# Nine buffers of arriving expert weights, taken from a free queue, in place of a ring of four

## The chip, the cores and the metric

The kernel runs on one core of one Trainium2 chip. The metric is the device time of one execution, in microseconds (us), lower is better. Before the change the median of three runs is 621.47 us (620.87 to 623.8). An execution with the hardware profiler gave the trace that is read here.

## The reference

Three parts follow one another. First an attention over 768 positions (2 batches, 8 heads of width 64) with 4 sink columns and a window of 128. Its output, 1536 tokens of 512 numbers, goes through an MLP with 2048 hidden units. The tokens then go to one of 8 experts each:

```
logits = x @ w_gate; e = argmax(logits); gate = softmax(logits)[e]
position of the token in its expert's queue (at most capacity = 384 = 1536/8*2)
h = relu(disp @ w1[e])          # 512 -> 1024
y = h @ w2[e]                   # 1024 -> 512
out[token] = gate * y           # zero for tokens beyond the capacity
```

All matrices of the experts are float32. Each expert has 2 MB in w1 and 2 MB in w2.

## The kernel before, in words

Attention, MLP and experts run one after the other; the order of the instructions of every engine is written out by hand (the scheduler is in manual mode for all five engines), and each engine runs its list in order. The change lies in the expert stage and in the loading of its weights.

**Weights.** The weights of an expert come in eight pieces of 128 x 1024 float32 (512 KB each): four of w1 ("up"), four of w2 ("down"); 64 pieces in all, in the order of `raw_src` (line 1126). A piece arrives in one of the four quarters of `raw_all` by a DMA on SP's queue (`raw_loads`, line 1160). `expert_split` (line 1141) then makes two tiles of it: ACT copies it to a rounded high part (line 1145), and VectorE (DVE) subtracts that from the piece for the low part (line 1147); for the last piece of an expert, GpSimd (POOL) subtracts in DVE's place. The two tiles lie in slots that were used by the earlier stages (32 slots, so the split weights of two experts fit). A quarter of `raw_all` is free again when its subtraction is done, so a load can be at most four pieces ahead of the splits. SP's queue holds nothing but these loads in this stage, and SP takes no part in the conditional blocks.

**Chunks.** An expert's tokens are worked on in chunks of 128: chunk 0 without a condition, chunks 1 and 2 in nested conditional blocks (`guard`, line 1196; `further_chunks`, line 1259), which PE, ACT, DVE and POOL run or skip by the counted tokens. A chunk is: fetch of the rows from the table `xs` in DRAM by POOL's queue (`fetch`, line 403); `turn_in` (line 411): four transposes on TensorE (PE), a copy on ACT, a subtraction on DVE; `expert_up` (line 1203): 24 matmuls and two ReLUs on ACT into `hh`; `turn_hidden` (line 1219): eight transposes, two copies on ACT into `hth` and two subtractions on DVE into `htl`; `expert_down` (line 1236): 24 matmuls, a scaling on DVE, and a scatter to the output by POOL. Three products (high-high, low-high, high-low) make each matrix product.

**Order in one expert e** (the loop at line 1285), as each engine sees its share of it:

```
splits_to((e + 1) * PER)              # four splits, down weights of e
expert_up(e, 0)
turn_in(e + 1, 0); turn_in(e, 1)
fetch(e + 2, 0); fetch(e + 1, 1)
splits_to((e + 1) * PER + PW1)        # four splits, up weights of e + 1
expert_down(e - 1, 0)
turn_hidden(e, 0)
further_chunks(e, 1)                  # conditional: chunks 1 and 2
fetch(e + 1, 2)
```

`raw_loads` is called after each group of splits. For expert 1 the groups are shifted by one piece, and for the last expert `turn_hidden(7, 0)` comes before `expert_down(6, 0)`. With the inputs measured, the conditional chunks that run are 1 and 2 of expert 0, 1 of expert 1, 1 of expert 3, and 1 and 2 of expert 6; experts 2, 4, 5 and 7 skip theirs. Chunk 0 of expert 0 is worked off among the last steps of the MLP.

**Room.** The pool `ep` (line 1182) opens when the MLP's pools are closed, in their memory. It has two buffers a tile unless a tile says otherwise: `hh` 2, `xha`/`xla` (chunk 0) and `xhb`/`xlb` (chunks 1, 2) 2 each, `hth` and `htl` 3 each.

Of the kernel before, what the change touches and what calls it, by code (L numbers as in the profile page):

```python
# [9 lines left out]
F32 = mybir.dt.float32  # L10
F32R = mybir.dt.float32r
# [24 lines left out]
def attention_mlp_moe_kernel(  # L36
# [17 lines left out]
    nc = tc.nc  # L54
    P = 128
    B, _, _, S = q.shape
    _, NG, _, GH, NQ, D1 = v.shape
    D = D1 - 1
    H = NG * GH
    NT, DM = out.shape  # L60
    DFF = w_in.shape[1]
    E = w_gate.shape[2]
    F = w1.shape[2]
# [7 lines left out]
    if n_sink == 0 and window == 0:  # L71
# [20 lines left out]
        out=lt, in_=lt, pattern=[[1, P]], compare_op=ALU.is_gt, fill=0.0,  # L92
# [22 lines left out]
    SW = 1024  # L115
# [69 lines left out]
    raw_all = rawpool.tile([P, 4 * SW], I32, name="raw_all")  # L185
# [215 lines left out]
    rows, tx, ep = {}, {}, []  # L401
# [9 lines left out]
    def turn_in(e, c, pt=None, th=None, tl=None):  # L411
        r = rows.pop((e, c))
        if pt is None:
            tag = "a" if c == 0 else "b"
            pt = next_bank("t")
            th = ep[0].tile([P, DM], F32R, tag=f"xh{tag}", name=f"xh{e}_{c}")
            tl = ep[0].tile([P, DM], F32R, tag=f"xl{tag}", name=f"xl{e}_{c}")
        for kk in range(KD):
            nc.tensor.transpose(pt[:, kk * P:(kk + 1) * P], r[:, kk * P:(kk + 1) * P], ident)
        nc.scalar.copy(th, pt)  # L420
        nc.vector.tensor_sub(tl, pt, th.bitcast(F32))
        tx[e, c] = (th, tl)

    def turn_in_slot(e, c, tag, pt):
        x = slot(tag)
        turn_in(e, c, pt, x[:, :DM], x[:, DM:])

    def first_chunk():
# [30 lines left out]
        for o in range(0, F, 512):  # L459
# [8 lines left out]
            yield  # L468
        splits_to(PER + PW1)
        raw_loads()  # L470
        got.extend((r, who, ht, downs))

# [17 lines left out]
    def mlp_steps():  # L490
# [30 lines left out]
        for bl in range(NBLK):  # L521
            last = bl == NBLK - 1
            if last:
                raw_loads()
                splits_to(1)
            for f in range(KF):
                n = bl * len(worder) + f
                conv = convert_at(n)
                next(conv, None)
                for ph in mlp_up(bl, f, wts[bl, "wi", f // FG]):  # L530
                    yield
                if last and f == KF - 1:
                    down_to(0)
                elif len(pending) == LAG:
                    routing = lower() or routing
                pending.append((bl, f, mlp_act(bl, f, ph, split_at(n), conv)))
                if f % 2 and bl == 1:
                    next(n_fill, None)
                if routing is not None and f >= 2:
                    next(routing, None)  # L540
                if last and f >= 2 and f % 2 and f < KF - 1:
                    splits_to(min(split_n[0] + 1, PER))
                    raw_loads()
                if last and f in (KF - 5, KF - 2):
                    next(first)
# [62 lines left out]
    with ExitStack() as actx:  # L608
# [19 lines left out]
        for i in range(NQ):  # L628
# [5 lines left out]
            m = ap_c.tile([P, w], F32, name=f"mask{len(masks)}")  # L634
# [3 lines left out]
            for (d, sink), o in zip(row, offs):  # L638
# [3 lines left out]
                if d * P - (P - 1) < 0:  # L642
                    nc.gpsimd.affine_select(
                        out=mb, in_=mb, pattern=[[-1, P]], compare_op=ALU.is_ge,
                        fill=NEG, base=d * P, channel_multiplier=1,
                    )
                if d * P + (P - 1) > window - 1:
                    nc.gpsimd.affine_select(
                        out=mb, in_=mb, pattern=[[1, P]], compare_op=ALU.is_ge,
# [264 lines left out]
        for n in range(nu + 11):  # L914
# [35 lines left out]
            if n == nu - EARLY:  # L950
                nc.vector.tensor_scalar(
                    out=nalpha, in0=alpha_sb, scalar1=-1.0, scalar2=None, op0=ALU.mult
# [23 lines left out]
    def moe_slot():  # L976
        moe_pos[0] += 1
        return slot(moe_tags[(moe_pos[0] - 1) % len(moe_tags)])
# [144 lines left out]
    w2_v = w2.rearrange("e (j p) d -> e p j d", p=P)  # L1123
    experts = {}

    raw_src = []

    def raw_of(m):
        return raw_all.bitcast(F32)[:, m % 4 * SW:(m % 4 + 1) * SW]

    for e in range(E):
        experts[e] = ([], [])
# [7 lines left out]

    def expert_split(m):
        _, dst, cut = raw_src[m]
        raw = raw_of(m)
        hi, lo = moe_slot(), moe_slot()
        nc.scalar.copy(hi, raw)  # L1145
        eng = nc.gpsimd if m % PER == PER - 1 and m > 2 * PER else nc.vector
        eng.tensor_sub(lo, raw, hi.bitcast(F32))  # L1147
        for o in range(0, SW, cut):
            dst.append([t[:, o:o + cut] for t in (hi, lo)])

    split_n, raw_n = [0], [0]

    def splits_to(n):
        while split_n[0] < min(n, len(raw_src)):
            if split_n[0] == raw_n[0]:
                raw_loads()
            expert_split(split_n[0])
            split_n[0] += 1

    def raw_loads():  # L1160
        while raw_n[0] < min(split_n[0] + 4, len(raw_src)):
            src = raw_src[raw_n[0]][0]
            nc.sync.dma_start(
                out=raw_of(raw_n[0]).rearrange("p (a b) -> p a b", a=src.shape[1]), in_=src
            )
            raw_n[0] += 1

    if not ahead:
# [18 lines left out]
    def next_bank(nm):  # L1187
        n = bank_n[nm] = bank_n.get(nm, -1) + 1
        return banks[nm][n % len(banks[nm])]

    counts, hid, hts = {}, {}, {}

    meta = ep[0].tile([P, E * NCH, 2], F32, name="meta", bufs=1)
# [9 lines left out]
    def expert_up(e, c):  # L1203
        ups = experts[e][0]
        x = tx.pop((e, c))
        h = ep[0].tile([P, F], F32, tag="hh", name=f"hh{e}_{c}")
        for o in range(0, F, 512):
            ph = next_bank("u")
            for kk in range(KD):
                for n, (xl, wl) in enumerate(((0, 0), (0, 1), (1, 0))):  # L1210
                    nc.tensor.matmul(  # L1211
                        ph, x[xl][:, kk * P:(kk + 1) * P],
                        ups[kk][wl][:, o:o + 512],
                        start=(kk == 0 and n == 0), stop=(kk == KD - 1 and n == 2),
                    )
            nc.scalar.activation(h[:, o:o + 512], ph, AF.Relu)  # L1216
        hid[e, c] = h

    def turn_hidden(e, c, between=None):
        h = hid.pop((e, c))  # L1220
        th = ep[0].tile([P, F], F32R, tag="hth", name=f"hth{e}_{c}", bufs=3)
        tl = ep[0].tile([P, F], F32R, tag="htl", name=f"htl{e}_{c}", bufs=3)
        hts[e, c] = (th, tl)
        for o in range(0, F, 512):
            w = slice(o, o + 512)
            pt = next_bank("t")
            for j in range(o // P, o // P + 4):
                nc.tensor.transpose(
                    pt[:, j * P - o:(j + 1) * P - o], h[:, j * P:(j + 1) * P], ident
                )  # L1230
            nc.scalar.copy(th[:, w], pt)
            nc.vector.tensor_sub(tl[:, w], pt, th.bitcast(F32)[:, w])
            if o == 0 and between:
                between()
# [24 lines left out]
    def further_chunks(e, c):  # L1259

        if c == NCH:
            return
        if NCH > 3:
            for c in range(1, NCH):
                with guard(e, c):
                    if c > 1:
                        fetch(e, c)
                        turn_in(e, c)
                    expert_up(e, c)
                    turn_hidden(e, c)  # L1270
                    expert_down(e, c)
            return
        with guard(e, c):  # L1273
            expert_up(e, c)
            turn_hidden(e, c, (lambda: turn_in(e, c + 1)) if c + 1 < NCH else None)
            expert_down(e, c)
            further_chunks(e, c + 1)

    nc.gpsimd.dma_start(
        out=meta, in_=xs.rearrange("(n p) d -> p n d", p=P)[:, :, DM:XW]  # L1280
# [4 lines left out]
    for e in range(E):  # L1285

        splits_to((e + 1) * PER - (e == 1))
        if e:
            expert_up(e, 0)
# [10 lines left out]
        if e == E - 1:  # L1300
            turn_hidden(e, 0)
# [84 lines left out]
```

## Time and profile before

| | |
|---|---|
| median of 3 runs | 621.47 us (620.87 to 623.8) |
| the profiled execution, its time | 619.51 us |
| its span, first to last instruction | 617.7 us |
| mean granted TensorE clock | 0.992 of full |
| attention, MLP and chunk 0 of expert 0 | 0 to 426 us |
| the rest of the expert stage | 427 to 612 us |
| PE busy over the span | 95% |
| weight loads of the experts | 64 of 512 KB, issued from 185.5 to 567.9 us |

How it is read: the profile gives, for each engine, what it ran and when, and for an instruction that began after an idle time, how long that was and what ended it. Times are us from the start of the span. A timeline row is start, duration, engine, line, operation, tile written <- tiles read, shape, count of instructions merged into the row, and in brackets the idle time before it and its releaser. "ACTq L1273" is ACT's instruction queue at the end of the loop body that holds the conditional blocks, not a computing instruction. The names `et`, `eo`, `es` are the PSUM banks of the expert stage, and `wi`, `wo`, `x`, `r` the slots of the split weights.

### The profile page before, as it was taken

The page shows a single profiled execution, that of the slowest core. Times are in us where ns is not written, and L with a number is a line of the kernel's source. Part 1 is how long each engine was busy: PE and PEld are TensorE (multiplying, and loading weights), DVE is VectorE, ACT ScalarE, POOL GpSimd, SP SyncE. Part 2 cuts the span into 40 slices and gives each one's busy share as a digit, 9 for nine tenths or more (in the row PEclk, how much of TensorE's full clock was granted, in tenths as well). Part 3 has the DMA queues.
Part 4 walks back from the last instruction along what each step waited for, and adds up shares of the span by engine and source line. Part 5 has one row for each costly group of instructions (what it writes and reads, how often), then busy time and mean ns, then how long its engine had stood idle before and what let it go on. Part 6 is the DMA issues. An engine that isn't in the chain of part 4 may idle for free. (4 is left out here: it accounts for less than half of the span.)

```text
span 617.7 us, 9115 instructions
## 1 busy us (share of the span) xinstructions
PE 589.9 (95%) x3230; PEld 493.4 (80%) x3230; DVE 400.6 (65%) x788; ACT 348.4 (56%) x642; POOL 98.3 (16%) x134
## 2 busy tenths in 40 slices
PE   7999999999999999999999999999999899889994
PEld 6999998888677888888899898876776687678783
DVE  6678788499998454444466787965146874766250
ACT  5668787475655544335465686835246564666330
POOL 5012333200000000002000110213120332222031
PEclk9999999999999999999999999999999999899999
DMA  7979731225568000001000012426345892999000
GB/s 221 303 238 298 206 122 69 69 84 190 162 195 324 1 1 0 2 17 52 0 2 1 36 49 69 154 73 216 99 129 179 289 329 90 315 319 314 24 21 34
DMA packets 32404, 81.76 MB, mean 132 GB/s; under 512 B 3574, under 2 KB 4134, under 8 KB 32352
## 3 DMA queue, kind: packets, MB, share of 16 engines
q1 hardware_dynamic: 28208, 69.54, 35.0%
q0 software_dynamic: 4144, 11.53, 5.4%
q8 instruction: 31, 0.51, 0.3%
q14 instruction: 21, 0.17, 0.1%
HBM read 66.65 MB, written 16.29 MB: 134 GB/s over the span
## 5 line engine op out<-in xcount | busy, mean ns | idle before, releaser
L350 PE MATMUL h<-x,r 128*128 128x512 f32 (+1 forms) x768 | 149.3, 341 | 3.2 <-DVE r L262 3.1
L350 PEld LDWEIGHTS h<-x,r 128*128 128x128 f32 x768 | 120.1, 189 | 22.3 <-DVE r L262 5.2
L381 PE MATMUL acc<-r,gh 128*128 128x512 f32 x384 | 120.6, 395 | 0.0
L381 PEld LDWEIGHTS acc<-r,gh 128*128 128x128 f32 x384 | 69.9, 188 | 14.4 <-ACT gh L370 0.3
L381 PE MATMUL acc<-r,gl 128*128 128x512 f32 x192 | 75.9, 395 | 0.0
L363 DVE SCALAR_TENSOR_TENSOR g<-gn,nalpha,g 128x512 f32<-128x512 f32 (+1 forms) x64 | 39.4, 616 | 47.5 <-ACT g L362 47.5
L722 PE MATMUL s<-ka,qa 128*128 128x260 f32 x192 | 59.8, 398 | 4.4 <-DMA qa<-in_q_dram 4.0
L361 ACT ACTIVATE gn<-h 128x512 f32<-128x512 f32 (+1 forms) x64 | 31.3, 490 | 53.5 <-PE h L350 53.2
L832 PEld LDWEIGHTS o<-vr,pT 128*128 128x128 f32 x352 | 55.6, 192 | 4.8
L1104 POOL DMA_INDIRECT xs<-x,slot_i x12 | 14.1, 1179 | 271.2 <-DVE run L1120 151.2
L262 DVE TENSOR_TENSOR r<-wo,r 128x1024 fp32r<-128x1024 f32 x31 | 38.0, 1224 | 27.6 <-ACT r L259 27.4
L832 PE MATMUL o<-vr,pT 128*128 128x65 f32 x352 | 53.6, 251 | 0.0
L1216 ACT ACTIVATE hh<-et 128x512 f32<-128x512 f32 x26 | 15.3, 596 | 59.5 <-PE et L1211 53.0
L741 ACT ACTIVATE p<-sx,mn 128x260 f32<-128x260 f32 (+1 forms) x96 | 42.9, 487 | 9.3 <-DVE mn L737 8.8
L259 ACT CAST r<-wo 128x1024 fp32r<-128x1024 f32 (+1 forms) x33 | 33.8, 1025 | 22.7 <-PE acc L381 21.7
L754 PE MATMUL pt<-ident,p 128*128 128x128 f32 x176 | 46.2, 278 | 0.0
L737 DVE CUSTOM_DVE_ANT_0 sx<-s,mask 128x260 f32<-128x260 f32 (+1 forms) x96 | 36.9, 401 | 13.7 <-PE s L722 8.5
L1147 DVE TENSOR_TENSOR wo<-raw_all,wi 128x1024 fp32r<-128x1024 f32 x29 | 39.5, 1392 | 9.2 <-ACT wi L1145 8.0
L370 ACT CAST gh<-g 128x512 fp32r<-128x512 f32 (+1 forms) x64 | 33.0, 515 | 21.3 <-DVE g L363 21.1
L381 PEld LDWEIGHTS acc<-r,gl 128*128 128x128 f32 x192 | 36.1, 188 | 8.6 <-DVE gl L373 0.2
L262 DVE TENSOR_TENSOR r<-wi,r 128x1024 fp32r<-128x1024 f32 x30 | 36.7, 1223 | 3.6 <-ACT r L259 3.4
L1145 ACT CAST wi<-raw_all 128x1024 fp32r<-128x1024 f32 x32 | 32.6, 1051 | 10.6 <-DMA raw_all<-in_w_dram 10.0
(192 smaller groups left out, 1106.9 us busy)
## 6 DMA issues: line engine op xcount, KB each, us to landing
raw_all<-in_w_dram SPq DMA_DIRECT2D x64, 512.0 KB, 5.2
raw_all<-in_w_in_dram SPq DMA_DIRECT2D x8, 1024.0 KB, 5.4
raw_all<-in_w_out_dram SPq DMA_DIRECT2D x8, 1024.0 KB, 5.0
xs<-r SPq DMA_DIRECT2D x8, 771.0 KB, 11.6
rows<-xs POOLq DMA_DIRECT2D x20, 256.0 KB, 4.7
vr<-in_v_dram SPq DMA_DIRECT2D x4, 780.0 KB, 4.9
out_dram<-fill SPq DMA_DIRECT2D x2, 1536.0 KB, 11.5
ka<-in_k_dram SPq DMA_DIRECT2D x7, 396.0 KB, 8.8
```

Source lines behind the costliest of these rows:

```text
L259: nc.scalar.copy(hi[:, x], w[:, x])
L262: eng.tensor_sub(lo[:, x], w[:, x], hi.bitcast(F32)[:, x])
L350: nc.tensor.matmul(ph[:, :TB], wi[wl][:, kk, f0:f0 + P], xT_at(kk, tok, TB, xl), start=(n == 0), stop=(n == 3 * KD - 1),)
L363: nc.vector.scalar_tensor_tensor(out=g, in0=gn, scalar=nalpha[:, f:f + 1], in1=g, op0=ALU.mult, op1=ALU.add)
L370: nc.scalar.copy(gh, g)
L381: nc.tensor.matmul(acc[t], g[a][:, t * P:(t + 1) * P], wo[w][:, f % FG, :], start=(f == 0 and x == 0), stop=(f == KF - 1 and x == 2),)
L722: nc.tensor.matmul(s[:, o:o + w], st.qa[:, h, toks], st.ka[:, c:c + w], start=True, stop=True, skip_group_check=True,)
L737: nc.vector.tensor_tensor_reduce(out=x[:, :w], in0=u.s[h][:, :w], in1=m[:, :w], scale=-scale, scalar=BIG, op0=ALU.add, op1=ALU.min, accum_ ...
L741: nc.scalar.activation(t.p[:, u.ii, h, :w], x[:, :w], AF.Exp, bias=t.mn[:, c:c + 1], scale=-1.0)
L754: nc.tensor.transpose(pt[:, c * P:(c + 1) * P], t.p[:, u.ii, h, u.offs[n]:u.offs[n] + P], ident,)
L832: nc.tensor.matmul(t.o[:, 2 * u.ii + h, :], u.pT[:, w], vr[:, hv * NQ + j, :], start=(not sg and n == 0), stop=(n == len(js) - 1), skip_gr ...
L1147: eng.tensor_sub(lo, raw, hi.bitcast(F32))
```

## The change

Five more buffers for arriving pieces (`more_raw`, 20 KB a partition) are allocated in `ep`, and the ring of four (piece m in quarter m mod 4) becomes a list of free buffers: a load takes the first free one, a split gives its buffer back to the end. Up to the opening of `ep` there are four buffers, as before; from there on nine. To make room, `hh`, `xha` and `xla` get one buffer instead of two, and `hth` and `htl` go from three buffers shared by all chunks to one for chunk 0 and one for chunks 1 and 2 (the other way round for the last expert): 16 KB a partition are given up.

```diff
-            th = ep[0].tile([P, DM], F32R, tag=f"xh{tag}", name=f"xh{e}_{c}")
-            tl = ep[0].tile([P, DM], F32R, tag=f"xl{tag}", name=f"xl{e}_{c}")
+            th = ep[0].tile([P, DM], F32R, tag=f"xh{tag}", name=f"xh{e}_{c}", bufs=1 + (c > 0))
+            tl = ep[0].tile([P, DM], F32R, tag=f"xl{tag}", name=f"xl{e}_{c}", bufs=1 + (c > 0))
...
+    MORE_RAW = 5
     raw_src = []
-    def raw_of(m):
-        return raw_all.bitcast(F32)[:, m % 4 * SW:(m % 4 + 1) * SW]
+    raw_free = [raw_all.bitcast(F32)[:, n * SW:(n + 1) * SW] for n in range(4)]
+    raw_at = {}
...
     def expert_split(m):
         _, dst, cut = raw_src[m]
-        raw = raw_of(m)
+        raw = raw_at.pop(m)
+        raw_free.append(raw)
...
     def raw_loads():
-        while raw_n[0] < min(split_n[0] + 4, len(raw_src)):
+        while raw_free and raw_n[0] < len(raw_src):
             src = raw_src[raw_n[0]][0]
-            nc.sync.dma_start(
-                out=raw_of(raw_n[0]).rearrange("p (a b) -> p a b", a=src.shape[1]), in_=src
-            )
+            raw = raw_at[raw_n[0]] = raw_free.pop(0)
+            nc.sync.dma_start(out=raw.rearrange("p (a b) -> p a b", a=src.shape[1]), in_=src)
             raw_n[0] += 1
...
+    more_raw = ep[0].tile([P, MORE_RAW * SW], F32, name="more_raw", bufs=1)
+    raw_free.extend(more_raw[:, n * SW:(n + 1) * SW] for n in range(MORE_RAW))
...
-        h = ep[0].tile([P, F], F32, tag="hh", name=f"hh{e}_{c}")
+        h = ep[0].tile([P, F], F32, tag="hh", name=f"hh{e}_{c}", bufs=1)
...
-        th = ep[0].tile([P, F], F32R, tag="hth", name=f"hth{e}_{c}", bufs=3)
-        tl = ep[0].tile([P, F], F32R, tag="htl", name=f"htl{e}_{c}", bufs=3)
+        tag = "b" if (c > 0) != (e == E - 1) else "a"
+        th = ep[0].tile([P, F], F32R, tag=f"hth{tag}", name=f"hth{e}_{c}", bufs=1)
+        tl = ep[0].tile([P, F], F32R, tag=f"htl{tag}", name=f"htl{e}_{c}", bufs=1)
```

## Rows read from the trace of the kernel before

**Rows 1.** The page, part 1: busy time, share of the span, instructions of each engine.

```profile
PE 589.9 (95%) x3230; PEld 493.4 (80%) x3230; DVE 400.6 (65%) x788; ACT 348.4 (56%) x642; POOL 98.3 (16%) x134
```

**Rows 2.** Stretches of 10 us; columns: PE, PEld, DVE, ACT, POOL, PEclk, DMA share, GB/s.

```profile
480.00:490.00 10.00, 9.93 (x51) 8.00 (x50) 7.68 (x6) 5.07 (x7) 3.60 (x4) 1.00 0.89 310
490.00:500.00 10.00, 7.31 (x27) 5.86 (x28) 7.48 (x8) 6.73 (x9) 2.08 (x3) 0.83 0.94 299
...
510.00:520.00 10.00, 10.00 (x49) 7.73 (x47) 1.89 (x4) 6.55 (x9) 0.13 (x1) 1.00 0.21 67
...
530.00:540.00 10.00, 7.66 (x31) 5.96 (x31) 7.27 (x9) 6.14 (x8) 1.58 (x2) 0.83 0.94 320
...
550.00:560.00 10.00, 8.38 (x45) 6.87 (x44) 7.39 (x9) 7.84 (x11) 3.12 (x3) 1.00 0.90 296
```

**Rows 3.** Timeline of PE in the expert stage.

```profile
468.73 0.66 PE L1228 MATMUL es<-ident,hh 128*128 128x128 f32 x4 [0.93 <-ACT hh L1216]
...
476.68 0.73 PE L1211 MATMUL et<-x,xh 128*128 128x512 f32 x2 [0.43 <-PEq L1273]
...
482.41 1.04 PE L419 MATMUL es<-ident,rows 128*128 128x128 f32 x8
...
488.89 1.03 PE L1228 MATMUL es<-ident,hh 128*128 128x128 f32 x8
492.69 0.80 PE L1211 MATMUL et<-wi,xh 128*128 128x512 f32 x1 [2.76 <-ACTq L1273]
...
499.77 1.03 PE L419 MATMUL es<-ident,rows 128*128 128x128 f32 x8
...
536.26 0.50 PE L1211 MATMUL et<-wi,xh 128*128 128x512 f32 x1 [2.34 <-ACTq L1273]
...
543.51 1.03 PE L419 MATMUL es<-ident,rows 128*128 128x128 f32 x8
...
552.66 0.72 PE L1211 MATMUL et<-x,xh 128*128 128x512 f32 x2 [1.62 <-ACTq L1273]
```

**Rows 4.** Timeline of ACT in the expert stage: splits (L1145) and copies of `hth` (L1231).

```profile
467.14 1.05 ACT L1145 CAST x<-raw_all 128x1024 fp32r<-128x1024 f32 x1 [1.62 <-DMA raw_all<-in_w_dram]
...
488.60 1.05 ACT L1145 CAST wi<-raw_all 128x1024 fp32r<-128x1024 f32 x1 [1.97 <-DMA raw_all<-in_w_dram]
490.57 1.04 ACT L1145 CAST wi<-raw_all 128x1024 fp32r<-128x1024 f32 x1 [0.93 <-DMA raw_all<-in_w_dram]
491.53 1.06 ACT L1231 CAST hth<-es 128x512 fp32r<-128x512 f32 x2
...
534.15 1.04 ACT L1145 CAST wi<-raw_all 128x1024 fp32r<-128x1024 f32 x1 [0.71 <-DMA raw_all<-in_w_dram]
535.10 1.06 ACT L1231 CAST hth<-es 128x512 fp32r<-128x512 f32 x2
...
551.49 1.07 ACT L1231 CAST hth<-es 128x512 fp32r<-128x512 f32 x2
```

**Rows 5.** Waits of SP's queue, 400 to 600 us (total us, times, longest).

```profile
SPq L1163 <- DVE wo L1147: 71.7, 26, 14.0
```

**Rows 6.** The page, part 6: DMA issues, KB each, us from issue to landing.

```profile
raw_all<-in_w_dram SPq DMA_DIRECT2D x64, 512.0 KB, 5.2
```

**Rows 7.** Stretches of 1 us; columns as in rows 2.

```profile
488.00:489.00 1.00, 1.00 (x6) 0.77 (x5) 0.00 (x0) 0.40 (x1) 0.00 (x0) 1.00 1.05 416
...
493.00:494.00 1.00, 1.00 (x3) 0.81 (x3) 1.00 (x2) 0.75 (x1) 0.00 (x0) 0.50 0.92 330
```

**Rows 8.** Timeline of DVE: subtractions of the splits, with and without POOL beside them.

```profile
521.41 5.70 DVE L1147 TENSOR_TENSOR wo<-raw_all,wi 128x1024 fp32r<-128x1024 f32 x3 [0.40 <-DVEq L1273]
...
529.13 2.36 DVE L1147 TENSOR_TENSOR wo<-raw_all,wi 128x1024 fp32r<-128x1024 f32 x2
```

**Rows 9.** Timeline of POOL: two fetches of rows.

```profile
483.31 1.09 POOL L409 DMA_DIRECT2D rows<-xs  x2 [0.78 <-PE es L419]
```

**Rows 10.** The tile `rows`, all 20 fetches.

```profile
DMA to landing us min/median/max: 2.9/4.7/6.5
```

## The prediction

> **What bounds the kernel now.** I began with the busy times: PE is busy for 95% of the span, the other engines for 65% or less [rows 1]. So only time in which PE stands still, or runs at a lower clock, can be won. The change touches the expert stage alone, and there the stretches of 10 us show where that time lies. Around 490 and 530 us PE is busy for 7.3 and 7.7 of 10 us, at a mean granted clock of 0.83; around 550 us for 8.4 at full clock [rows 2]. In the same stretches DMA is 0.90 to 0.94 busy at about 300 GB/s, while between 510 and 520 us, with PE fully busy, it moves only 67 GB/s. The loads come in bursts beside the stalls and pause between them.
>
> Next, PE's timeline: what ended each idle time. Three times PE waited ahead of `expert_up` (L1211): 2.76, 2.34 and 1.62 us, ended each time by ACT's queue passing the end of the loop body that holds the conditional blocks (ACTq) [rows 3]. These are the starts of experts 3, 5 and 6, each after an expert whose chunks 1 and 2 are skipped. Where the chunk before was run (expert 2 at 476.68) the wait is 0.43. My reading: the PSUM bank that `expert_up` fills was last read by a ReLU in a conditional block, so PE may go on only when ACT has passed that block. ACT's timeline says why ACT was late: just ahead of it stand the two copies of `turn_hidden` (L1231), and ahead of these the splits of the next expert's up weights, the last of which waited 0.93 us (after 1.97) and 0.71 us for their pieces [rows 4]. The copies end at 491.53 + 1.06 = 492.59 and PE goes on at 492.69; at 535.10 + 1.06 = 536.16, and PE at 536.26; at 551.49 + 1.07 = 552.56, and PE at 552.66. It is the same 0.10 us three times, so the chain is weights, split, copies, conditional block, PE.
>
> Last, why the pieces are late: SP waited 71.7 us in 26 waits for DVE to free a quarter of the ring [rows 5], and a load takes 5.2 us to land [rows 6]. With a ring of four, the loads of the pieces needed at 528 us can't start before the subtractions of the four before them, which begin at 521.41 [rows 8]; DMA stood idle until then.
>
> **The change part by part.** *Five more buffers.* No instruction is added or taken away; 48 of the 64 loads may start up to five pieces earlier. In the pause around 515 us the pieces for the next splits then land before ACT asks for them. ACT's waits for DMA go, and ACT reaches the two copies before PE has made the transposes that they read. What is left of a stall: PE ends the transposes, at 488.89 + 1.03 = 489.92 [rows 3]; ACT copies the second half (half of the pair's 1.06, so 0.53) and passes the block (0.10): about 0.65, taken as 0.7 us. It is at most 1.2, if both copies begin only then. It is 0 only if PE could pass without ACT, which the order forbids, but I keep 0 as the far end.
> - Idle time: (2.76 - 0.7) + (2.34 - 0.7) + (1.62 - 0.7) = 4.6 us.
> - Clock: behind the two long stalls the granted clock is 0.50 of full, the 1.2 GHz level [rows 7]. `expert_up`, with nothing else in it, took 492.69 to 499.77 = 7.08 us and 536.26 to 543.51 = 7.25 us, against 476.68 to 482.41 = 5.73 us at full clock [rows 3]. Won: 1.35 + 1.52 = 2.9 us. After the stall of 1.62 the clock stayed at 1.00 (stretch from 550 us, rows 2), so one of 0.7 should cost none.
> - Expert 1: PE waited 0.93 us for a ReLU at 468.73 [rows 3]; ACT came late to it behind a split that had itself waited 1.62 for its piece [rows 4]. With the piece there, the ReLU is on time: 0.9 us.
>
> Sum: 4.6 + 2.9 + 0.9 = **8.4 us**. With 1.2 us left at each stall it is 8.4 - 1.5 = 6.9, with nothing left 8.4 + 2.1 = 10.5.
>
> *Who is late next?* ACT: eight splits of 1.05 [rows 4] and three pairs of half copies of 1.06 make 11.6 us per skipped expert. PE needs 5.73 + (489.92 - 482.41) + 0.7 = 13.9 us, so ACT keeps up. DVE: its four subtractions of up weights began at 529.13 and cost 2.36 / 2 = 1.18 each [rows 8], so without waits they end at 533.9, and PE goes on at about 536.26 - 2.34 + 0.7 = 534.6: free, with 0.7 us of cover (the later pieces are also needed later). DMA: a skipped expert needs eight pieces, three fetches of 256 KB and one output of 256 KB, 5.2 MB. At 320 GB/s, the best stretch with stalls [rows 2], that takes 16.4 us; at the 416 of one microsecond of loads alone [rows 7] 12.6. At the low rate the supply falls back by 2.5 us or 0.8 MB, some 1.5 pieces, per skipped expert. Five pieces in reserve bear three such experts in a row; at most two (4 and 5) follow one another, and chunk 1 of expert 3 gives time to refill. So I cost DMA at nothing.
>
> *Buffers given up.* `hh`, `xha`, `xla`, `hth`, `htl`: the writer of each waits for PE's last read of the old content. In every case the writer (ACT or DVE) reads a PSUM bank that PE fills after that last read in its own order: `hh` is read by transposes ahead of the next `expert_up`; `xha` by the `expert_up` ahead of the next `turn_in`; `hth` of chunk 0 by `expert_down(e - 1, 0)`, just ahead of `turn_hidden(e, 0)`. For the last expert, whose `turn_hidden` comes first, the change swaps the two tags. So no new wait can end last: nothing. If that cover were missing, one wait would cost up to a full `expert_up`, 5.73 us.
>
> *First loads into the new room.* They wait for the old tenants, which end with the MLP; SP has nothing else queued. Up to five more loads then run beside the first fetches and the table of gates: 5 x 512 KB at 416 GB/s = 6.3 us of DMA, during 26 us of PE work on expert 0's chunks with little DMA. I put nothing on it.
>
> *Fetches of rows.* These come by POOL's queue, beside more loads. Today they land after 2.9 to 6.5 us [rows 10], with up to four loads on the way; with as many more as the reserve has, this can grow, but 12.9 us remain until they are used (rival D works that out), so I cost it at nothing. The Trainium skill (DMA: Bandwidth & Descriptors, Queues, rings and completion order) says that each DMA engine takes turns between the queues at packets; by that a fetch isn't put behind the whole queue of loads, and rival D falls. No row of this trace shows a fetch behind nine loads, so D stays.
>
> **The rivals.** *A, DMA still binds.* The share of 0.94 [rows 2] speaks for it: the reserve is used up, and expert 5's stall with its clock loss and expert 6's stay: 8.4 - (1.64 + 1.52 + 0.92) = 4.3 us won, 617.2 us. Against it: 67 GB/s between the bursts.
>
> *B, PE's wait was not the weights'.* ACT is late at the copies for a reason of its own, and only expert 1's 0.9 us comes: 620.6 us. The DMA waits right ahead of the copies speak against it.
>
> *C, the change doesn't do what it says*: the loads stay four ahead, since the new room comes free late or SP is held: 621.5 us. SP's list holds only loads, and nothing in it depends on the conditional blocks.
>
> *D, slower: late rows.* The fetches at 483.31 [rows 9] are used by `turn_in` at 499.77. In the new order an expert takes 13.9 us and its fetch starts some 1 us after the last `turn_in`, so 12.9 us remain. If a fetch came behind nine loads (9 x 512 KB at 320 to 416 GB/s is 11.3 to 14.7 us, and 2.9 for itself), it would land 14.2 to 17.6 us after issue: PE waits 1.3 to 4.7 us, say 3, at five experts, 15 us: 621.5 - 8.4 + 15 = 628 us. It decides only from a landing of 12.9 us on, twice the longest seen; and loads are given out one at a time as DVE frees buffers, so nine rarely stand in line.
>
> **How the numbers follow.** The sum belongs to the profiled execution, 619.51 us with a span of 617.7; it lies 2 us below the median of 621.47, as runs differ. I take the difference over in us: 621.5 - 8.4 = **613.1 us**. Chances: forecast 0.71, A 0.12, B 0.07, C 0.04, D 0.06. The forecast's bounds give 611.0 to 614.6; the runs before lay 0.6 below to 2.3 above their median, which makes 610 to 617. The range takes in A with 2 us of that: 610 to 619.5, leaving out C, D and most of B. About 0.5%, 3.1 us, is what a measurement of this kernel can tell from no change. Faster by more: the forecast and nearly all of A, 0.82. Within: B, C and the rest of A, 0.12. Slower: D, 0.06.
>
> **What would show it.** Right: between 470 and 560 us the splits (L1145) no longer wait for DMA; PE's idle times ahead of L1211 fall to 0.6 to 1.2 us with ACTq as their end; the clock stays at 1.00; DMA works through the pause around 515 us, and the last load is issued earlier than before. Wrong: splits that still wait for DMA at experts 5 and 6 (A); the same stalls with no DMA wait ahead of the copies (B); PE waiting at `turn_in` for rows (D).

## The result, and the profile after

| | before | after |
|---|---|---|
| median | 621.89 us (620.87 to 623.8, 4 runs) | 611.99 us (611.73 to 612.21, 4 runs) |
| profiled execution | 619.51 us | 612.21 us |
| its span | 617.7 us | 610.4 us |
| mean granted clock | 0.992 | 0.997 |

The ratio is 0.9837, with a 95% interval of 0.9812 to 0.9862: faster by 9.9 us, and the four runs lie within 0.5 us of each other, where those before spread over 2.9. Line numbers have moved by up to 6: the matmul of `expert_up`, L1211, is now L1214, the two steps of a split are L1147 and L1149, the copies of `hth` L1237. L1273, the line at which [rows 3] name ACT's queue as PE's releaser, is now L1279. It reads `with guard(e, c)`: it opens the conditional block, and is not the end of the loop body.

Busy times first, the page's part 1. PE runs the same 3230 matmuls; its busy time is 2.5 us shorter than in [rows 1], about what the two `expert_up` that ran at half clock gain (1.23 and 1.53 us, below).

```profile
PE 587.4 (96%) x3230; PEld 491.7 (81%) x3230; DVE 396.6 (65%) x788; ACT 346.6 (57%) x642; POOL 100.0 (16%) x134
```

PE's timeline, as in [rows 3]. The three idle times of 2.76, 2.34 and 1.62 us are 0.77 each, still ended by ACT's queue. `expert_up` takes 496.38 - 490.53 = 5.85 and 537.03 - 531.31 = 5.72 us, where it took 7.08 and 7.25.

```profile
476.51 0.73 PE L1214 MATMUL et<-x,xh 128*128 128x512 f32 x2 [0.42 <-PEq L1279]
...
488.73 1.04 PE L1234 MATMUL es<-ident,hh 128*128 128x128 f32 x8
490.53 0.50 PE L1214 MATMUL et<-wi,xh 128*128 128x512 f32 x1 [0.77 <-ACTq L1279]
...
496.38 1.03 PE L419 MATMUL es<-ident,rows 128*128 128x128 f32 x8
...
517.27 0.73 PE L1214 MATMUL et<-x,xh 128*128 128x512 f32 x2 [0.43 <-PEq L1279]
...
531.31 0.50 PE L1214 MATMUL et<-wi,xh 128*128 128x512 f32 x1 [0.77 <-ACTq L1279]
...
537.03 1.03 PE L419 MATMUL es<-ident,rows 128*128 128x128 f32 x8
...
545.33 0.73 PE L1214 MATMUL et<-x,xh 128*128 128x512 f32 x2 [0.77 <-ACTq L1279]
```

ACT's timeline, as in [rows 4]. Splits run one behind the other without a wait, and the copies now wait for PE's transposes (1.59 us) instead of coming late to them. 489.36 + 1.07 = 490.43, and PE goes on at 490.53: the same 0.10 us as before.

```profile
484.82 2.96 ACT L1147 CAST wi<-more_raw 128x1024 fp32r<-128x1024 f32 x3
489.36 1.07 ACT L1237 CAST hth<-es 128x512 fp32r<-128x512 f32 x2 [1.59 <-PE es L1234]
...
527.49 1.06 ACT L1147 CAST wi<-more_raw 128x1024 fp32r<-128x1024 f32 x1
530.14 1.07 ACT L1237 CAST hth<-es 128x512 fp32r<-128x512 f32 x2 [1.59 <-PE es L1234]
```

ACT's waits from 470 to 560 us, all of them (total, times, longest): none is for a load.

```profile
ACT hh L1219 <- PE et L1214: 22.7, 9, 4.7
ACT hth L1237 <- PE es L1234: 7.9, 5, 1.6
ACT wi L1147 <- ACTq L1279: 0.5, 2, 0.3
```

Stretches of 10 us, columns as in [rows 2]. PE runs at full clock throughout. DMA still pauses while chunk 1 of expert 3 runs, and more than before (20 GB/s from 510 to 520 us, where it was 67): SP issues no load between 503.77 and 519.28 us, since all nine buffers hold pieces that came before the pause. After it DMA moves up to 387 GB/s. Before, the best of these stretches in the expert stage was not the 320 of [rows 2] but 354, in this row:

```profile
500.00:510.00 10.00, 10.00 (x53) 8.31 (x52) 8.04 (x9) 6.72 (x9) 3.83 (x4) 1.00 0.95 354
```

After:

```profile
490.00:500.00 10.00, 9.47 (x44) 7.71 (x45) 7.13 (x9) 8.25 (x12) 5.50 (x5) 1.00 0.98 360
...
510.00:520.00 10.00, 9.57 (x44) 7.16 (x43) 4.60 (x6) 5.52 (x8) 1.56 (x2) 1.00 0.06 20
...
530.00:540.00 10.00, 9.23 (x46) 7.45 (x45) 7.24 (x10) 8.23 (x12) 5.55 (x5) 1.00 1.00 351
540.00:550.00 10.00, 9.23 (x44) 7.37 (x43) 9.76 (x10) 8.04 (x10) 2.26 (x3) 1.00 1.03 387
```

Where the time came from, by the start of `expert_up` of each expert in the two timelines (the expert stage begins at 427.53 before, 428.61 after; its last scatter at 610.94 and 603.65):

| from, to | before | after | won | forecast |
|---|---|---|---|---|
| start of the stage, expert 2 | 49.15 | 47.90 | 1.25 | 0.9 (a late ReLU) |
| expert 2, 3 | 16.01 | 14.02 | 1.99 | 2.06 (stall) |
| expert 3, 4 | 27.96 | 26.74 | 1.22 | 1.35 (clock) |
| expert 4, 5 | 15.61 | 14.04 | 1.57 | 1.64 (stall) |
| expert 5, 6 | 16.40 | 14.02 | 2.38 | 1.52 (clock) + 0.92 (stall) |
| expert 6, last scatter | 58.28 | 58.32 | 0.0 | 0 |
| sum | | | 8.4 | 8.4 |

Between these two executions the sum is the forecast one. That it meets it to a tenth is in part luck: expert 1 brought 0.35 us more, the other rows together 0.37 less. The spans differ by 7.3 us only, since the stage begins 1.1 us later after the change; nothing ahead of the stage was changed. The medians differ by 9.9 us, 1.5 more than the sum; experiment 4 is about that.

### The profile page after: what moved, and what is told of

It reads as the page before. It is cut to its first block, busy times and chain, and to the rows that moved or that the text cites. A ratio compares the mean times of both kernels' runs of the same rounds, so it can differ in the third digit from the quotient of the medians.

```text
span 610.4 us, 9113 instructions
## 1 busy us (share of the span) xinstructions
PE 587.4 (96%) x3230; PEld 491.7 (81%) x3230; DVE 396.6 (65%) x788; ACT 346.6 (57%) x642; POOL 100.0 (16%) x134
## 5 line engine op out<-in xcount | busy, mean ns | idle before, releaser
L373 DVE TENSOR_TENSOR gl<-g,gh 128x512 fp32r<-128x512 f32 (+1 forms) x64 | 35.3, 551 | 1.6 <-ACT gh L370 1.6
L722 PEld LDWEIGHTS s<-ka,qa 128*128 128x128 f32 x192 | 31.2, 201 | 5.6 <-issue 4.2
```

The source lines that it names most:

```text
L373: nc.vector.tensor_sub(gl, g, gh.bitcast(F32))
L722: nc.tensor.matmul(s[:, o:o + w], st.qa[:, h, toks], st.ka[:, c:c + w], start=True, stop=True, skip_group_check=True,)
```

## The experiments

Theory W is that of the prediction. The name `after` stands for the changed kernel.

**1. The room without the buffers** (`e1_room_only`):

```diff
-    MORE_RAW = 5
+    MORE_RAW = 0
```

> The changed kernel without the five added buffers: hh, xh, xl, hth and htl have the few buffers of after, the pieces of weights arrive in the old four, through the free list. Theory W (the gain is the weights' earlier arrival): as before the change, 621.9 us within 0.5%, the stalls of 2.8, 2.3 and 1.6 us ahead of expert_up back, ACT's splits waiting for DMA again. Rival T (the new tags and places of the intermediate tiles bring the gain, or part of it): 612 us, or between. If the tiles with one buffer cost something that the gain hides, it is slower than before: over 623.

Measured: 621.3 us, ratio to before 1.0005 (0.9975 to 1.0036). The stalls are back, in this execution 3.02, 2.05 and 2.80 us on PE's timeline:

```profile
493.20 0.78 PE L1215 MATMUL et<-wi,xh 128*128 128x512 f32 x1 [3.02 <-ACTq L1280]
...
536.65 0.50 PE L1215 MATMUL et<-wi,xh 128*128 128x512 f32 x1 [2.05 <-ACTq L1280]
...
554.25 0.87 PE L1215 MATMUL et<-x,xh 128*128 128x512 f32 x2 [2.80 <-ACTq L1280]
```

Behind each of the three, `expert_up` takes 7.26 or 7.27 us, at half clock. What follows: the tiles with fewer buffers and the free list, which this kernel also has, cost and bring nothing beyond the interval's 0.3%; the gain comes from the five added buffers. Rival T falls.

**2 and 3. One and two added buffers** (`e2_five_buffers`, `e3_six_buffers`): `MORE_RAW = 1` and `MORE_RAW = 2`, otherwise as after.

> One added buffer in place of five. In the trace before, ACT waited for the third and fourth piece of the up weights (to about 488.6 and 490.5, 532.4 and 534.1 us), while PE's transposes ended at 489.9 and 533.9. With one load more ahead each piece lands about when the one before it did, so the fourth would be split at about 489.6 and 533.4, just in time. Theory W, limit by latency: 613 to 615 us, stalls of 0.8 us at experts 3 and 5, perhaps 1 to 1.6 at expert 6, which follows another skipped expert. Rival P (the gain grows with each buffer up to nine, since DMA's rate binds and only the reserve helps): a fifth of 9.9 us, 620 us, with two long stalls left.

> Two added buffers in place of five. Theory W: 612 to 613 us, as with five, all three stalls at 0.8 us, no wait for DMA ahead of the copies of turn_hidden. Rival P: two fifths of the gain, 618 us.

Measured: 613.36 us with one added buffer (five in all), ratio 0.9864 (0.9813 to 0.9915); 611.86 us with two added (six in all), 0.9852 (0.98 to 0.9905), not to be told from nine. The timeline of PE with five in all; this execution took 616.68 us, the others 612.41 to 613.57:

```profile
491.04 0.50 PE L1215 MATMUL et<-wi,xh 128*128 128x512 f32 x1 [1.00 <-ACTq L1280]
...
532.39 0.51 PE L1215 MATMUL et<-wi,xh 128*128 128x512 f32 x1 [1.34 <-ACTq L1280]
...
548.36 1.20 PE L1215 MATMUL et<-x,xh 128*128 128x512 f32 x2 [2.70 <-ACTq L1280]
```

With one added buffer two stalls fall most of the way (1.00 and 1.34 us, where 0.8 was expected). The third, behind a second skipped expert in a row, is longer than I expected (2.70 against at most 1.6), so there a second piece of reserve does count. With six in all the three stalls are 0.77 us, as with nine, and ACT's waits for loads from 470 to 560 us are down to four, none ahead of the copies of experts 2, 4 and 5, which wait for PE (total, times, longest):

```profile
ACT hth L1238 <- PE es L1235: 7.1, 5, 1.6
ACT wi L1147 <- DMA raw_all<-in_w_dram: 0.6, 1, 0.6
ACT x L1147 <- DMA more_raw<-in_w_dram: 0.6, 2, 0.3
...
ACT r L1147 <- DMA raw_all<-in_w_dram: 0.5, 1, 0.5
```

Three of the five buffers bring nothing that can be measured. Rival P falls: what was short was a start one or two pieces earlier, not a large reserve.

**4. The kernel before, profiled again** (`e4_before_again`), without an edit.

> The kernel before, profiled once more. Its first profiled execution took 619.5 us, the runs without a profile had a median of 621.9 and spread over 2.9 us, while the changed kernel's four lie within 0.5. If the rest of 1.5 us between the sum of 8.4 and the measured 9.9 is the clock (a stall of 1.6 to 2.8 us sometimes lowers it and sometimes not, at up to 1.5 us each), this profile shows another number of stretches at 0.5 of full clock than two, or one of another length. If it shows the same two and the same time, the rest lies outside the expert stage.

Measured: 621.9 us in its one execution, a span of 620.0. PE's timeline around expert 6, then stretches of 1 us (columns as in rows 2):

```profile
553.40 0.73 PE L1211 MATMUL et<-x,xh 128*128 128x512 f32 x2 [1.82 <-ACTq L1273]
...
560.65 1.03 PE L419 MATMUL es<-ident,rows 128*128 128x128 f32 x8
```

```profile
556.00:557.00 1.00, 1.00 (x3) 0.74 (x3) 1.00 (x2) 0.72 (x2) 0.48 (x1) 0.50 0.91 340
```

Here the third stall, 1.82 us long, lowers the clock too, to the 1.2 GHz level: `expert_up` of expert 6 takes 560.65 - 553.40 = 7.25 us. It took 558.37 - 552.66 = 5.71 in the first profile, where the stall was 1.62 and the clock stayed. So the profile on which I made the sum had two such losses, this one and that of experiment 1 have three. The third is worth 1.5 us, and 8.4 + 1.5 is the 9.9 us between the medians. The table's rows, made for this execution, say the same: from the start of the stage to the last scatter it took 613.23 - 428.49 = 184.74 us, against 603.65 - 428.61 = 175.04 after, 9.7 us more. That the runs without a profile mostly had three losses is an inference, but each has a granted clock on record. The profile with two losses has a mean of 0.992, this one with three 0.989, the changed kernel with none 0.997. Of 54 executions of the kernel before that were taken beside the experiments, 12 show 0.992 or more, with a median of 618.7 us, and 25 show 0.989 or less, with a median of 622.9 (a 55th, at 625.6 us and 0.986, is left out). The 54 spread over 8.2 us, 14 of the changed kernel, at 0.995 to 0.997, over 2.1.

**5. ACT made late** (`e5_act_late`):

```diff
+    late = ep[0].tile([P, 256], F32, name="late", bufs=1)
+    nc.gpsimd.memset(late, 0.0)
...
+        if e:
+            for _ in range(4):
+                nc.scalar.copy(late, late)
         further_chunks(e, 1)
```

> The changed kernel with four extra copies of 128 x 256 on ACT (0.27 us each, some 1.1 us) for experts 1 to 7, between the two copies of turn_hidden(e, 0) and the conditional blocks. Nothing reads their result. Theory W says that PE, ahead of expert_up of the next expert, waits until ACT has passed the block: the stalls at experts 3, 5 and 6 grow from 0.77 to about 1.9 us, together 3.2 us, 615.2 us, and up to 1.5 more for each at which the clock falls. Where the chunk runs, ACT waits for PE there anyway, and nothing is lost. Rival Q (PE waits for the copies, DVE or the weights, and ACT's queue only happens to be there): 612 us, stalls at 0.77.

Measured: 622.84 us, ratio to before 1.0033 (1.0005 to 1.0062); the whole gain is gone. ACT's timeline at expert 2, then PE's at experts 1 to 6:

```profile
491.49 1.07 ACT L1239 CAST hth<-es 128x512 fp32r<-128x512 f32 x2 [1.59 <-PE es L1236]
492.45 1.73 ACT L1329 COPY late<-late 128x256 f32<-128x256 f32 x4
```

```profile
470.74 0.66 PE L1236 MATMUL es<-ident,hh 128*128 128x128 f32 x4 [0.96 <-ACT hh L1221]
...
494.37 0.50 PE L1216 MATMUL et<-wi,xh 128*128 128x512 f32 x1 [2.47 <-ACTq L1281]
...
500.09 1.03 PE L419 MATMUL es<-ident,rows 128*128 128x128 f32 x8
...
536.98 0.50 PE L1216 MATMUL et<-wi,xh 128*128 128x512 f32 x1 [2.75 <-ACTq L1281]
...
554.25 1.04 PE L1216 MATMUL et<-x,xh 128*128 128x512 f32 x2 [2.47 <-ACTq L1281]
...
561.51 1.03 PE L419 MATMUL es<-ident,rows 128*128 128x128 f32 x8
```

The copies cost 1.73 us, not 1.1 (a copy that reads what the one before wrote takes 0.405 us). 0.77 + 1.73 = 2.50: the stalls grew by the whole of it at two places (2.47), and by a little more at the third (2.75). Nothing reads the copies, so the wait ends when ACT has passed the block; rival Q falls. The time is above my 615 to 619.7. From the start of the stage to the last scatter this execution took 10.05 us more than the profiled one of the changed kernel: the stalls account for 2.47 + 2.75 + 2.47 - 2.31 = 5.4 us, two losses of clock, at experts 5 and 6 (561.51 - 554.25 = 7.26 us), for 3.1, and the stretch up to expert 2 for 1.7. That last part I had put at nothing; 0.96 of it is shown: at expert 1, whose chunk runs, ACT came late to a ReLU behind the copies, and PE waited for it (470.74).

**6. Banks that no conditional block touches** (`e6_own_banks`):

```diff
-    banks = {"t": every[:3], "u": every[3:6], "y": every[6:]}
+    banks = {"t": every[:3], "u": every[3:5], "v": every[5:7], "y": every[7:]}
...
-            ph = next_bank("u")
+            ph = next_bank("v" if c else "u")
...
-        py = next_bank("y")
+        py = next_bank("u" if (e, c) == (E - 1, 0) else "y")
```

> The changed kernel with other PSUM banks: expert_up of chunk 0 has two banks of its own, that of chunks 1 and 2 two others (three were shared by all), and expert_down has one in place of two (the last expert's takes one of expert_up's). No instruction in a conditional block then reads the banks that expert_up of chunk 0 fills. If the reading of the wait as one for the bank is right, the stalls of 0.77 us at experts 3, 5 and 6 go, down to the 0.43 us that the start of an expert costs after a chunk that ran, or to nothing: 1.0 to 2.3 us won, 609.7 to 611.0 us. If PE waits for ACT for another reason (a count of ACT's events that is complete only behind the block), nothing moves: 612 us. If the single bank of expert_down costs: slower by 0.7 us for each wait.

Measured: 616.89 us, ratio 0.9929 (0.9901 to 0.9956), slower than the changed kernel beside it (612.79, `e7_after_again`, 0.9854). The three stalls did go, to 0.15 at experts 3 and 5 and to nothing that shows at 6, but a new one stands at the start of the stage, on PE's timeline:

```profile
433.22 1.09 PE L419 MATMUL eo<-ident,r 128*128 128x128 f32 x4 [5.12 <-DVEq L1319]
...
497.80 0.47 PE L1214 MATMUL et<-wi,xh 128*128 128x512 f32 x1 [0.15 <-PEq L1279]
```

That was my mistake, and the same mechanism on another engine: line 1319 is the conditional block of expert 0's first chunk, whose `expert_down` took the one bank "y". The next user, `turn_in_slot`, had to wait for DVE to pass that block, and PE then ran at half clock up to 439 us.

> The changed kernel once more, beside the one with other banks: 611 to 613 us, the stalls of 0.77 us three times, full clock throughout the expert stage.

Measured: 612.79 us (0.9812 to 0.9896 around 0.9854), three stalls of 0.77 us.

**8. The same, with that bank mended** (`e8_own_banks_2`):

```diff
-        py = next_bank("u" if (e, c) == (E - 1, 0) else "y")
+        py = next_bank("u" if c == 0 and e in (0, E - 1) else "y")
```

> As the kernel with other PSUM banks, but the conditional work of expert 0's first chunk takes a bank of expert_up in expert_down, so that the one bank of expert_down is touched by no conditional block when the first turn_in of expert 1 needs it. The wait of 5.12 us at 433 us, ended by DVE's queue passing that block, should fall to the 0.78 us of before, and with it the 7 us at half clock behind it. With the three stalls at 0.15 as in that run: 612.4 - 3 x 0.62 = 610.5 us, faster than the changed kernel by 1 to 2.5 us. If the wait at 433 us has another cause, it stays at 616.9.

Measured: 610.38 us, ratio to before 0.9819 (0.9792 to 0.9846). The wait ahead of `turn_in_slot` is back at 0.78 us, and the clock stays at 1.00 behind it; no wait of PE ends at ACT's queue any more.

```profile
427.53 0.66 PE L419 MATMUL eo<-ident,r 128*128 128x128 f32 x4 [0.78 <-ACT x L484]
```

**10 and 11. After and this version side by side** (`e10_after_beside`, `e11_banks_beside`):

> The changed kernel, on the same chip as the next run: 611 to 613 us, three stalls of 0.77 us at experts 3, 5 and 6.

> The changed kernel with the second set of PSUM banks once more, beside the changed kernel on the same chip, since the two ratios taken on different chips have intervals that overlap. If the 0.6 us at each of three stalls are real, it is 1 to 2.5 us faster than the run before it, 609.5 to 611.5 us; if it was the chip, the two are within 0.5 us.

Measured: after 612.34 us (611.3 to 612.63), 0.9873 (0.9845 to 0.99); with the banks 609.35 us (608.72 to 610.86), 0.9831 (0.9806 to 0.9855). The runs of the two do not overlap: 3.0 us won between the medians, 2.5 between the spans of the two profiled executions (609.5 and 607.0), where the stalls make 2.3. What the rest is was not found. PE's longest waits from 420 to 612 us in the second (total, times, longest); there is none for ACT's queue left:

```profile
PE et L1214 <- PEq L1279: 0.9, 2, 0.4
PE eo L419 <- ACT x L484: 0.8, 1, 0.8
PE es L1234 <- DVE xl L421: 0.6, 1, 0.6
```

**9. The banks without the buffers** (`e9_before_banks`): the bank lines of 6, with that of 8, in the kernel before.

> The kernel before (ring of four, old tiles) with these PSUM banks alone. Theory W has two links: the pieces come late, and PE waits for ACT to pass the block behind the last split and the copies. Without the second link PE needs the pieces one by one: at expert 3 in the trace before, the last low part was ready at 492.9 and would be needed at about 492.4, at experts 5 and 6 at 536.45 and 552.85, needed at about 536.4 and 553.5. So the stalls fall below 0.7 us though ACT still waits for DMA: 612 to 615 us. If the pieces' lateness alone is what costs (the block only shows it), the stalls stay above 1.5 us and the time is 617 us or more.

Measured: 617.11 us (614.23 to 622.32), ratio 0.9917 (0.9885 to 0.9949): about half the gain. The time lies at the edge of the second forecast, the stalls between the two. The profiled execution took 622.32 us, more than any other of this kernel, so it shows more waiting than the median; PE's timeline at experts 3 and 6:

```profile
489.77 0.47 PE L1211 MATMUL et<-wi,xh 128*128 128x512 f32 x1 [0.15 <-PEq L1273]
492.89 0.50 PE L1211 MATMUL et<-wi,xh 128*128 128x512 f32 x1 [0.78 <-issue]
...
554.22 0.80 PE L1211 MATMUL et<-x,xh 128*128 128x512 f32 x1 [2.82 <-ACT x L1145]
```

At experts 3 and 5 the stall is gone, as worked out. Within `expert_up` of expert 3 PE stands still for 0.78 us; the profile names no releaser for it ("issue"), so that this is the wait for the last low part is not shown. At expert 6 PE, no longer held back, comes to the last pieces before they are there, and waits 2.82 us for the split itself. So both links are real: the late pieces cost without the block, and the block makes them cost more.

## Why the prediction was right

*What bounds it, and the chain.* Right, and shown: experiment 1 takes the buffers away and the stalls return, 5 lengthens them by way of ACT's queue alone, 6 and 8 remove them by way of the banks. My reading of the bank as what ties PE to the block is thereby more than a reading. [Rows 4] showed the late pieces for two of the three stalls; the trace of before has them for the third as well, ahead of the copies at 551.49:

```profile
550.54 1.04 ACT L1145 CAST x<-raw_all 128x1024 fp32r<-128x1024 f32 x1 [1.11 <-DMA raw_all<-in_w_dram]
```

The 71.7 us of [rows 5] are only the waits for the subtractions into `wo`; with those into `x` and `r`, SP waited 124.9 us for DVE's subtractions.

*Where the loads go.* Wrong in a detail: I said that the pieces for the splits at 528 us would land in the pause around 515 us, and gave a working DMA there as a sign. They landed before it, and DMA moved less in the pause than before (20 GB/s against 67). The reserve was full by then, which serves the splits as well.

*Five more buffers: idle time.* Right in size: 0.77 us are left at each stall, taken as 0.7.

*Clock.* The mechanism was right, the term was mis-sized for the median. I counted two losses, 2.9 us, since "after the stall of 1.62 the clock stayed at 1.00", as if that were so in every run. In the profiles of experiments 1 and 4 the third stall lowers the clock as well; with it the term is 4.4 us and the sum 9.9. I had seen that the profiled execution lay 2 us below the median and put it down to "as runs differ". The granted clocks in experiment 4 point to the same cause as that of the term itself.

*Expert 1.* 0.9 forecast, 1.25 measured for the whole stretch, and the stall of 0.93 is gone.

*Who is late next.* Nobody, as costed: ACT's copies wait 1.6 us for PE, and from 470 to 560 us no split waits for a load. DMA at nothing was right, but its two prices were not good ones. 320 GB/s was too low, as the 354 of the same trace show. The 416 was not a microsecond of loads alone: 0.12 of its 0.42 MB came by the queue of the row fetches and outputs. By the 5.2 MB that I counted for a skipped expert, one every 14.02 us takes 374 GB/s, and 351 and 387 were moved from 530 to 550 us. So rival A does not come here, where two skipped experts follow one another and six buffers already do what nine do; that DMA would keep up with a longer row of them isn't shown.

*Buffers given up.* Nothing, as said (1.0005 in experiment 1). *Rivals B, C* fall with the ACT waits above, and the last load is issued at 550.0 us, where it was 567.9. *Rival D:* the fetches of rows land little later than in [rows 10]:

```profile
DMA to landing us min/median/max: 3.0/5.7/6.8
```

1 us more in the median and 0.3 in the longest, far from the 12.9 us at which they would decide. The Trainium skill's rule (DMA: Bandwidth & Descriptors, Queues, rings and completion order) that an engine takes turns between queues agrees with this, though this is no test of it: how deep the queue of loads was at each fetch was not measured.

## What to carry to other kernels

A wait that an engine's queue ends at a conditional block (ACTq, DVEq at the line of the block) can be a dependency on work that was skipped: in both cases here a PSUM bank was shared with the block. Try giving the unconditional work a buffer of its own there. Give the loads that feed the chain a buffer or two of reserve; here two sufficed and five cost nothing. Where the profiled execution differs from the median by as much as one of the terms, look for the term that comes and goes, by profiling the same kernel twice and by the granted clocks of the other runs.

## What the runs showed of the hardware

Whether a pause of PE lowers its clock to the 1.2 GHz level isn't told by the length of that pause alone: one of 1.62 us did not, 1.82 and 2.05 did (experiments 4 and 1), and in experiment 5 a pause of 2.47 us at expert 3 did not (500.09 - 494.37 = 5.72 us for `expert_up`) while one of 2.47 at expert 6 did (7.26 us). What decides between them is open. Each loss costs 1.2 to 1.5 us here.

With nine buffers DMA moved 387 GB/s over 10 us, loads, row fetches and outputs together, against 354 at best with four. The busy share isn't a measure of what is left: 0.94 stood beside 299 and 320 GB/s [rows 2], 0.95 beside 354, and 1.03 beside 387.
